# k^T v of batches 2 to 7 made one batch per token tile instead of all in the first tile, in linear attention with a feed-forward layer

## The chip, the cores and the metric

The kernel runs on one core of a Trainium2 chip. The metric is the device time of one execution in microseconds (us); less is better. The core's engines work side by side, each through its own list of instructions in order: TensorE (PE, with its weight loads as PEld), VectorE (DVE), ScalarE (ACT), GpSimd (POOL), and SyncE (SP), which here issues nearly all DMAs. They wait for each other by semaphores. Matrix products land in PSUM; ACT and DVE carry them on to SBUF.

## The reference

q, k, v have the shape (8 batches, 8 heads, 576 positions, 64), all float32. For each batch and head:

```python
kv = np.einsum('bhsd,bhse->bhde', k, v)
out = np.einsum('bhsd,bhde->bhse', q, kv)
rms = np.sqrt(np.mean(out * out, axis=-1, keepdims=True) + 1e-06)
x = out / rms * g_norm            # then heads side by side: (4608, 512)
h = x @ w_in                      # w_in (512, 2048)
g = h * np.tanh(softplus(h))      # "Mish"
return g @ w_out                  # w_out (2048, 512)
```

w_in and w_out are float64 in memory, so the kernel reads them as pairs of 32-bit words and builds float32 values from them.

## The kernel before

**Tiles and slots.** The 4608 tokens are cut into nine tiles of 512 (NT = 9). A tile lies over one or two batches (576 positions each), which `segments(j)` tells. The first half of the kernel makes h and g of every tile and stores g in DRAM (`gd`); the second half loads g and multiplies it with w_out. Both products use a scheme in which a 2 by 2 block product takes seven multiplications of blocks (A11, S1, ... with B11, T1, ...) instead of eight. Each factor is split into a high and a low part of the fast matmul type, and each product is three matmuls (low by high, high by low, high by high). In the first half one multiplication is 12 matmuls of 128x128 by 128x256 (L478) and fills one *slot*. A tile has four groups of seven, so NS = 28 slots; tile i has the slots 28 i to 28 i + 27.

**A plan by slots.** The order is written out by hand. `at(t, f)` puts a piece of work behind the product of slot t, `then(t, f)` ahead of it; `slot` runs both lists. Within a slot the pieces run in the order in which they were registered, and every engine and SP's DMA queue keep that order. A slot below zero is put at slot 0. What comes before slot 0 is a preamble, written line by line.

**w_in.** It comes in eight chunks j, each of four DMAs of 256 KB (L135) into one buffer (`w64`, a single one; chunk 1 has a room of its own). Then SCALE (ACT, L140), JOIN (three DVE instructions, L145 to L147, after which the buffer is free for the next load), DIFF (DVE, L155 to L157), BLOCKS and SUMS (casts on ACT, L118, with a subtraction on DVE, L119). A chunk j from 2 on has LOAD at slot 3(j-2)-2 (chunk 2's is in the preamble), SCALE and JOIN at 3(j-2), DIFF and BLOCKS one later, SUMS two later. Group n of tile 0 needs the chunks 2n and 2n+1. w_out is converted in 16 pieces of the same steps, from tile 1 on, every 12 slots.

**k^T v.** `kv_product` makes the product of one or two pairs of heads: 20 float32 matmuls with 64 columns each per pair (L233), into one PSUM bank `kvps`, whose halves go by the batch's parity. Batch 0 is done in the preamble. The 28 pairs of batches 1 to 7 stand at slots 0 to 20 of tile 0; each pair needs four DMAs (`km`, `kr`, `vm`, `vr`, L212 and L213) into one of two buffers (`kvp`), and the load of a pair is issued two pairs ahead. `kv_keep` copies a finished batch to SBUF with ACT (L245). `kv_store` then puts it into DRAM (`kvd`), and from tile 2's attention on, `kv_fetch` and `kv_split` bring it back and split it into a high and a low part.

**Attention.** The attention of tile j runs during tile j-1, in two units of four heads: load of q (8 DMAs, L286), transpose (DVE, L291), halves (the split), project (q by k^T v, L314 or L317 to L319), square, scaled, squares, sums (L349 to L352), rstd (ACT), keep and spread (rstd to DRAM and back, spread over partitions, L367 and L374), normalize (DVE, L382). `x_form` then makes the split left factors of the next tile (slots 24 to 32). Tiles 0 and 1 (T32 = 2) use plain float32 matmuls, which need no halves.

**Stores.** `put_in` applies Mish on ACT and stores g two or three slots later from SP (L496, L501, L504).

The names and lines that matter below: `kv_keep`, `kv_store`, `kv_fetch`, `kv_split` (L243 to L258), `project` (L304), the preamble (L528 to L590), the planned slots of w_in and of k^T v (L593 to L604), `attention` (L606), and the slots of w_out's conversion (L651 to L661).

Of the kernel before, what the change touches and what calls it, by code (L numbers as in the profile page):

```python
# [26 lines left out]
def linear_attention_rms_mish_ffn(  # L27
# [33 lines left out]

# [32 lines left out]
    kvs = part1.enter_context(tc.tile_pool(name="kvs", bufs=1))  # L94
    xp = part1.enter_context(tc.tile_pool(name="xp", bufs=1))
# [13 lines left out]
    kvd = [tc.dram_tile([P, NKC, P], F32, name=f"kvd{b}") for b in range(B)]  # L109
# [107 lines left out]
    def kv_staging():  # L217
        ts = []
        for name in ("k", "v"):
            ts.append(pools["kvp"].tile([P, 2, CM * D], F32, name=f"{name}m"))  # L220
            ts.append(pools["kvp"].tile([SL, 2, D], F32, name=f"{name}r"))
        return ts
# [14 lines left out]
    kvf = [kvs.tile([P, 2, NKC, P], F32, name=f"kv{n}") for n in range(2)]  # L237
    kvt = {}

    def kv_room(b):  # L240
        return kvf[0][:, b] if b < 2 else kvf[1][:, b % 2]

    def kv_keep(b, n):  # L243
        for r in (slice(0, D), slice(D, P)):
            nc.scalar.copy(kv_room(b)[r, n, r], kvps[r, b % 2, n, :])  # L245

    def kv_store(b):
        nc.sync.dma_start(kvd[b], kv_room(b))

    raw = {}  # L250

    def kv_fetch(b):
        raw[b] = kvs.tile([P, NKC, P], F32, name="kvr")
        nc.sync.dma_start(raw[b], kvd[b])

    def kv_split(b):
        kvt[b] = kvs.tile([P, 2, NKC, P], F32R, name=f"kv{b % 2}")
        split(kvt[b][:, 0], kvt[b][:, 1], raw[b])  # L258
# [14 lines left out]
    def unit_steps(j, u):  # L273
# [30 lines left out]
        def project():  # L304
# [208 lines left out]
    open_pools(wst, ("w64", 1), ("wd", 1), ("kvp", 2))  # L513
# [32 lines left out]
    staged = []  # L546
# [351 lines left out]
```

## Time and profile before

| | us |
|---|---|
| median of 3 runs (957.92 to 959.98) | 958.29 |
| the profiled execution | 959.49 |
| its span, first to last instruction | 957.7 |
| PE busy | 853.3 (89%) |
| DVE busy | 610.0 (64%) |
| ACT busy | 463.2 (48%) |
| DMA of SP's queue, share of 16 engines | 61.1% |

The page's second part cuts the span into 40 slices of 24 us. A digit is the busy share of the slice in tenths; PEclk is the clock that TensorE was granted, in the same tenths:

```profile
PE   3468758999979999997989969999999999999997
DVE  2476442768668676748585515886766777667762
ACT  1444333666646666655666525444444434444341
PEclk9667978999999999998999989999999999999999
DMA  9478987667659768765873799634544345443331
```

The first slot begins in the second slice, the second half of the kernel at about the 25th (587 us). In a row of the timeline, the first number is the start, the second the length, both in us; several instructions of one line are merged (x12), and in brackets stand the idle time ahead and what ended it. "SPq" is a DMA being issued by SP, not its transfer. In a row of groups, "busy, mean ns of one" and the idle time before it follow after the bars.

### The profile page before, as it was taken

What the parts mean: (1) busy time and instruction counts of PE and PEld (TensorE: products, weight loads), DVE (VectorE), ACT (ScalarE), POOL (GpSimd) and SP (SyncE); (2) the same over time, 40 slices, a digit from 0 to 9 for tenths busy, and PEclk for the clock granted to TensorE, in tenths of its full rate; (3) what the DMA queues carried; (4) which work ended last, traced back from release to release, by engine and by line L of the source; (5) the groups of instructions that cost most, each with busy time, mean ns of one, the idle gap of its engine ahead of it and who ended that gap; (6) DMA issues with size and microseconds to landing.
All of it is one profiled execution on the core that took longest, in us unless ns stands there. A gap on an engine that the chain in (4) does not pass through costs nothing.

```text
span 957.7 us, 17048 instructions
## 1 busy us (share of the span) xinstructions
PE 853.3 (89%) x6940; PEld 811.8 (85%) x6940; DVE 610.0 (64%) x801; ACT 463.2 (48%) x703; POOL 3.4 (0%) x19
## 2 busy tenths in 40 slices
PE   3468758999979999997989969999999999999997
PEld 1156546989879989887989969999999999999997
DVE  2476442768668676748585515886766777667762
ACT  1444333666646666655666525444444434444341
POOL 1000000000000000000000000000000000000000
PEclk9667978999999999998999989999999999999999
DMA  9478987667659768765873799634544345443331
GB/s 250 114 197 231 268 257 216 225 203 234 190 171 276 221 181 255 221 184 155 241 208 132 244 405 367 217 111 141 165 124 123 110 120 168 134 130 110 111 111 45
DMA packets 159150, 181.08 MB, mean 189 GB/s; under 512 B 18976, under 2 KB 138784, under 8 KB 158048
## 3 DMA queue, kind: packets, MB, share of 16 engines
q1 hardware_dynamic: 155872, 177.64, 61.1%
q10 hardware_dynamic: 3200, 2.36, 1.0%
q8 instruction: 54, 0.88, 0.4%
q14 instruction: 24, 0.20, 0.1%
HBM read 116.13 MB, written 63.83 MB: 188 GB/s over the span
## 4 chain that ended last, share of the span: by engine, by line
PE 62%; DMA 12%; DVE 11%; ACT 7%; SPq 4%; issue 3%; ACTq 0%; DVEq 0%
PE a L726 20%; PE bc L726 15%; PE a L478 11%; PE bc L478 7%; DMA vm<-in_v_dram 3%; DMA gd<-ula 3%; PE q L808 2%; PE s L233 2%; DMA w<-in_moe_w_in_dram 2%; DMA gd<-ur 2%; DMA qs<-in_q_dram 2%; DVE ur L498 1%; DVE fl L119 1%; ACT gf L118 1%; SPq L135 1%
## 5 line engine op out<-in xcount | busy, mean ns | idle before, releaser
L726 PE MATMUL a<-wf,gf 128*128 128x256 f32 x1632 | 201.8, 283 | 0.5 <-DVE ur L757 0.5
L726 PEld LDWEIGHTS a<-wf,gf 128*128 128x128 f32 x1632 | 198.4, 192 | 0.7 <-DVE ur L757 0.7
L478 PE MATMUL a<-gf,wf 128*128 128x256 f32 x1296 | 179.9, 295 | 17.2 <-DVE gf L380 10.9
L478 PE MATMUL bc<-gf,wf 128*128 128x256 f32 x1296 | 176.8, 291 | 15.0 <-DVE ula L498 7.6
L119 DVE TENSOR_TENSOR gf<-g,gf 128x1024 fp32r<-128x1024 f32 (+1 forms) x123 | 132.9, 1087 | 87.9 <-ACT gf L118 87.8
L478 PEld LDWEIGHTS a<-gf,wf 128*128 128x128 f32 x1296 | 169.3, 201 | 21.7 <-issue 11.7
L478 PEld LDWEIGHTS bc<-gf,wf 128*128 128x128 f32 x1296 | 167.1, 197 | 17.5 <-issue 9.0
L118 ACT CAST gf<-g 128x1024 fp32r<-128x1024 f32 (+1 forms) x123 | 114.5, 939 | 90.5 <-DVE g L706 65.3
L726 PE MATMUL bc<-wf,gf 128*128 128x256 f32 x1224 | 152.6, 283 | 0.1
L726 PEld LDWEIGHTS bc<-wf,gf 128*128 128x128 f32 x1224 | 149.4, 192 | 0.3 <-ACT gf L118 0.3
L478 PEld LDWEIGHTS a<-a,wf 128*128 128x128 f32 x432 | 57.3, 199 | 9.1 <-DVE ur L498 4.8
L115 ACT ACTIVATE ur<-ur 128x1024 f32<-128x1024 f32 x36 | 38.1, 1058 | 53.4 <-DVE ur L498 53.4
L478 PE MATMUL a<-a,wf 128*128 128x256 f32 x432 | 61.0, 293 | 1.9 <-DVE ur L498 1.8
L233 PE MATMUL s<-vm,km 128*64 128x64 f32 x448 | 24.3, 266 | 32.7 <-DMA vm<-in_v_dram 20.7
L233 PEld LDWEIGHTS s<-vm,km 128*64 128x64 f32 x448 | 20.1, 172 | 37.6 <-DMA vm<-in_v_dram 10.3
L498 DVE TENSOR_TENSOR ula<-bc,ula 128x512 f32<-128x512 f32 x36 | 24.7, 686 | 35.6 <-PE bc L478 18.2
L446 ACT COPY ur<-bc 128x512 f32<-128x512 f32 (+1 forms) x53 | 27.5, 518 | 39.2 <-PE bc L726 23.0
L118 ACT CAST gf<-gf 128x512 fp32r<-128x512 f32 x45 | 27.8, 618 | 38.2 <-DVE gf L404 18.2
L118 ACT CAST gf<-a 128x1024 fp32r<-128x1024 f32 x17 | 17.9, 1051 | 53.4 <-DVE a L703 53.4
L119 DVE TENSOR_TENSOR gf<-gf 128x512 fp32r<-128x512 f32 x45 | 31.0, 689 | 17.3 <-ACT gf L118 16.7
L455 ACT COPY ur<-a 128x512 f32<-128x512 f32 (+1 forms) x53 | 27.4, 517 | 30.2 <-PE a L726 24.6
L119 DVE TENSOR_TENSOR fl<-fa,fh 128x1024 fp32r<-128x1024 f32 x28 | 34.1, 1219 | 9.4 <-ACT fh L118 9.4
(129 smaller groups left out, 867.7 us busy)
## 6 DMA issues: line engine op xcount, KB each, us to landing
g<-gd SPq DMA_DIRECT2D x18, 2048.0 KB, 8.7
gd<-ur SPq DMA_DIRECT2D x36, 512.0 KB, 5.1
wod<-wst SPq DMA_DIRECT2D x16, 896.0 KB, 5.4
wf<-wod SPq DMA_DIRECT2D x8, 1792.0 KB, 15.0
gd<-ula SPq DMA_DIRECT2D x36, 256.0 KB, 4.4
gd<-ulb SPq DMA_DIRECT2D x36, 256.0 KB, 4.6
w<-in_moe_w_out_dram SPq DMA_DIRECT2D x32, 256.0 KB, 5.1
w<-in_moe_w_in_dram SPq DMA_DIRECT2D x28, 256.0 KB, 4.5
```

The costliest lines, as they stand in the source:

```text
L115: nc.scalar.activation(o, i, AF.Mish)
L118: nc.scalar.copy(hi, src)
L119: nc.vector.tensor_sub(lo, src, hi.bitcast(F32))
L135: nc.sync.dma_start(dst, src)
L233: nc.tensor.matmul(kvps[o * D:(o + 1) * D, b % 2, h0 // 2 + i, :], kt, vt, start=(c == 0), stop=(c == CM))
L446: then(t + 2, lambda: nc.scalar.copy(dst(st, "22"), st["c"]))
L455: then(t + 4, lambda: nc.scalar.copy(dst(st, "12"), st["a"]))
L478: nc.tensor.matmul(bank[:, jj], w[:, right, a, kc, :], xf[:, b, kc, :], start=first and jj == kc == s == 0, stop=(kc == 1 and s == 2), ski ...
L498: nc.vector.tensor_add(o, bank, o)
L726: nc.tensor.matmul(bank, gf[:, a, c, :], wo[c][:, right, b, :], start=first and c == s == 0, stop=(c == NF2 - 1 and s == 2), skip_group_ch ...
L808: nc.tensor.matmul(banks[b][:, h], gf[:, a, c, :], wo[2 * n + c][:, right, d, :], start=n == c == s == h == 0, stop=last_one, skip_group_c ...
```

## The change

- k^T v of batch 1 stays at the start of tile 0, one pair per slot (0 to 3). Batch b from 2 on has its four pairs at the slots 13, 16, 19 and 22 of tile b-2, that is, two tiles ahead of the attention which first needs it. Its first two loads are issued at slots 20 and 23 of the tile before (batch 2: at 4 and 6), the other two at 14 and 17.
- `kv_keep` writes the split parts straight from PSUM at slot 24 (slot 4 for batch 1); the trip through DRAM (`kv_store`, `kv_fetch`, `kv_split`) is gone. Batches 0 and 1 have their float32 tiles in the pool `kvf`, which closes with tile 0; the staging buffers `kvp` stay open.
- w_in: SCALE and JOIN of chunk 2 move from the preamble into slot 0, and the load of chunk j+1 is at slot 3(j-2)+1, as before, but chunk 2's stands earlier in SP's order. In the preamble w_in's first load stands ahead of k's and v's, DIFF and SUMS of chunk 0 stand earlier, and g_norm's load stands later.
- Attention: q's first load at -19 (was -18), transpose at -1 (0), halves at 0 (1), the second unit's load at 1 (2), keep at 17 (18), spread at 19 (20), normalize at 24 and 25 (23 and 24), the x forms at 25 to 30 and 32 (24, 25 and 28 to 32). For tile 1's attention the steps ahead of 19 come two slots later.
- w_out's conversion begins two slots later (NS+6 instead of NS+4), and its loads are 13 slots ahead instead of 16.

```diff
@@ -92,6 +91,7 @@
     ps_t = part1.enter_context(tc.tile_pool(name="ps_t", bufs=1, space=PSUM))
     att = part1.enter_context(tc.tile_pool(name="att", bufs=1))
     kvs = part1.enter_context(tc.tile_pool(name="kvs", bufs=1))
+    kvp = part1.enter_context(tc.tile_pool(name="kvp", bufs=2))
     xp = part1.enter_context(tc.tile_pool(name="xp", bufs=1))
     wst = part1.enter_context(ExitStack())
     pools = {}
@@ -106,7 +106,6 @@
     sel = const.tile([P, NKC, H], F32R, name="sel")
     gd = [tc.dram_tile([P, NFC, T], F32, name=f"gd{i}") for i in range(NT)]
     wod = [tc.dram_tile([P, 7, 2, G], F32, name=f"wod{c}") for c in range(NF2)]
-    kvd = [tc.dram_tile([P, NKC, P], F32, name=f"kvd{b}") for b in range(B)]
     rd = [tc.dram_tile([H, T], F32, name=f"rd{j}") for j in range(NT)]
 
     ctx.enter_context(tc.manual_schedule(engines=None))
@@ -217,8 +216,8 @@
     def kv_staging():
         ts = []
         for name in ("k", "v"):
-            ts.append(pools["kvp"].tile([P, 2, CM * D], F32, name=f"{name}m"))
-            ts.append(pools["kvp"].tile([SL, 2, D], F32, name=f"{name}r"))
+            ts.append(kvp.tile([P, 2, CM * D], F32, name=f"{name}m"))
+            ts.append(kvp.tile([SL, 2, D], F32, name=f"{name}r"))
         return ts
 
     kvps = ps_t.tile([P, 2, NKC, D], F32, name="s2")
@@ -234,28 +233,23 @@
 
 
 
-    kvf = [kvs.tile([P, 2, NKC, P], F32, name=f"kv{n}") for n in range(2)]
-    kvt = {}
-
-    def kv_room(b):
-        return kvf[0][:, b] if b < 2 else kvf[1][:, b % 2]
+    kvf, kvt = [], []
+
+    def kv_tiles():
+        for n in range(T32):
+            kvf.append(pools["kvf"].tile([P, NKC, P], F32, name=f"kvf{n}"))
+            nc.gpsimd.memset(kvf[n], 0.0)
+        for n in range(2):
+            kvt.append(kvs.tile([P, 2, NKC, P], F32R, name=f"kv{n}"))
+            nc.gpsimd.memset(kvt[n].bitcast(F32), 0.0)
 
     def kv_keep(b, n):
         for r in (slice(0, D), slice(D, P)):
-            nc.scalar.copy(kv_room(b)[r, n, r], kvps[r, b % 2, n, :])
-
-    def kv_store(b):
-        nc.sync.dma_start(kvd[b], kv_room(b))
-
-    raw = {}
-
-    def kv_fetch(b):
-        raw[b] = kvs.tile([P, NKC, P], F32, name="kvr")
-        nc.sync.dma_start(raw[b], kvd[b])
-
-    def kv_split(b):
-        kvt[b] = kvs.tile([P, 2, NKC, P], F32R, name=f"kv{b % 2}")
-        split(kvt[b][:, 0], kvt[b][:, 1], raw[b])
+            if b < T32:
+                nc.scalar.copy(kvf[b][r, n, r], kvps[r, b % 2, n, :])
+        for r in (slice(0, D), slice(D, P)):
+            if b >= T32 - 1:
+                split(kvt[b % 2][r, 0, n, r], kvt[b % 2][r, 1, n, r], kvps[r, b % 2, n, :])
 
 
     def segments(j):
@@ -311,9 +305,9 @@
                 ps, hp = st["x"][a], 2 * u + a
                 for b, _, c in segments(j):
                     if j < T32:
-                        nc.tensor.matmul(ps[:, c], kvf[0][:, b, hp, :], st["q"][:, a, c], start=True, stop=True)
+                        nc.tensor.matmul(ps[:, c], kvf[b][:, hp, :], st["q"][:, a, c], start=True, stop=True)
                         continue
-                    kh, kl, qh, ql = kvt[b][:, 0, hp, :], kvt[b][:, 1, hp, :], st["qh"][:, a, c], st["ql"][:, a, c]
+                    kh, kl, qh, ql = kvt[b % 2][:, 0, hp, :], kvt[b % 2][:, 1, hp, :], st["qh"][:, a, c], st["ql"][:, a, c]
                     nc.tensor.matmul(ps[:, c], kl, qh, start=True, stop=False)
                     nc.tensor.matmul(ps[:, c], kh, ql, start=False, stop=False)
                     nc.tensor.matmul(ps[:, c], kh, qh, start=False, stop=True)
@@ -510,7 +504,7 @@
         for s in steps:
             units[j][u][s]()
 
-    open_pools(wst, ("w64", 1), ("wd", 1), ("kvp", 2))
+    open_pools(wst, ("w64", 1), ("wd", 1), ("kvf", 1))
     rooms = [up.tile([P, 4, CM * D], F32, name="ur") for _ in range(2)]
     rooms += [x[:, 2 * u:2 * u + 2].rearrange("p a (h n) -> p (a h) n", h=2) for u in range(2)]
     rrooms = [up.tile([SL, 4, D], F32, name=n) for n in ("ula", "ula", "ulb", "ulb")]
@@ -525,15 +519,20 @@
         for s in steps:
             conv[j][s]()
 
-    kv0 = [kv_load(nc.scalar, 0, 4 * n, 4, [t for m in range(2) for t in (rooms[2 * n + m], rrooms[2 * n + m])]) for n in range(2)]
+    staged = {}
+
+    def k_load(b, p):
+        staged[b, p] = kv_load(nc.sync, b, 2 * p, 2, kv_staging())
+
+    def k_product(b, p):
+        kv_product(b, 2 * p, 2, *staged.pop((b, p)))
+
     nc.scalar.preload_act_table_set("natural_log_exp_and_others")
     weights(0, LOAD)
+    kv0 = [kv_load(nc.scalar, 0, 4 * n, 4, [t for m in range(2) for t in (rooms[2 * n + m], rrooms[2 * n + m])]) for n in range(2)]
     do(0, 0, "load")
     weights(1, LOAD)
-    for r in (slice(0, D), slice(D, P)):
-        nc.sync.dma_start(gcol[r, :], g_norm.rearrange("(p o) -> p o", o=1))
-    for t in kvf:
-        nc.gpsimd.memset(t, 0.0)
+    kv_tiles()
     nc.gpsimd.memset(eps, 1e-6)
     nc.gpsimd.memset(ones, 0.0)
     nc.gpsimd.memset(ones[0:D, 0:D], 1.0)
@@ -543,37 +542,24 @@
         for o in range(2):
             nc.gpsimd.memset(sel[o * D:(o + 1) * D, hp, 2 * hp + o:2 * hp + o + 1].bitcast(F32), 1.0)
 
-    staged = []
-    order_kv = [(b, h0) for b in range(1, B) for h0 in range(0, H, 2)]
-
-    def kv_next_load():
-        if order_kv:
-            b, h0 = order_kv.pop(0)
-            staged.append((b, h0, kv_load(nc.sync, b, h0, 2, kv_staging())))
-
-    def kv_next_product(t):
-        b, h0, ts = staged.pop(0)
-        kv_product(b, h0, 2, *ts)
-        if h0 == H - 2:
-            then(t + 1, lambda: kv_keep(b, slice(0, NKC)))
-            at(t + 3, lambda: kv_store(b))
-
     weights(0, SCALE, JOIN)
     kv_product(0, 0, 4, *kv0[0])
     kv_keep(0, slice(0, 2))
+    weights(0, DIFF)
     do(0, 0, "transpose")
     do(0, 1, "load")
-    kv_next_load()
-    kv_next_load()
-    weights(0, DIFF)
+    for r in (slice(0, D), slice(D, P)):
+        nc.sync.dma_start(gcol[r, :], g_norm.rearrange("(p o) -> p o", o=1))
+    weights(2, LOAD)
+    k_load(1, 0)
     do(0, 0, "project")
+    weights(0, BLOCKS)
     kv_product(0, 4, 4, *kv0[1])
     kv_keep(0, slice(2, 4))
-    weights(0, BLOCKS)
     do(0, 0, "square", "sums")
+    weights(0, SUMS)
     do(0, 1, "transpose", "project", "square")
-    weights(0, SUMS)
-    weights(2, LOAD)
+    k_load(1, 1)
     do(0, 0, "rstd")
     do(0, 1, "sums")
     weights(1, SCALE, JOIN)
@@ -586,7 +572,6 @@
     x_form(S1)
     weights(1, SUMS)
     x_form(S2)
-    weights(2, SCALE, JOIN)
     x_form(A12)
 
 
@@ -595,70 +580,56 @@
     at(2, lambda: x_form(A22))
     for j in range(2, NF2):
         t = 3 * (j - 2)
-        for s, n in ((LOAD, -2), (SCALE, 0), (JOIN, 0), (DIFF, 1), (BLOCKS, 1), (SUMS, 2)):
-            if j > 2 or s >= DIFF:
-                at(max(t + n, 0), lambda j=j, s=s: weights(j, s))
-    for n in range(len(order_kv) + len(staged)):
-        t = n * 6 // 8
-        at(t, lambda t=t: kv_next_product(t))
-        at(t, kv_next_load)
+        if j + 1 < NF2:
+            at(t + 1, lambda j=j: weights(j + 1, LOAD))
+        for s, n in ((SCALE, 0), (JOIN, 0), (DIFF, 1), (BLOCKS, 1), (SUMS, 2)):
+            at(t + n, lambda j=j, s=s: weights(j, s))
+
+
+    for p in range(4):
+        if p > 1:
+            at(p - 2, lambda p=p: k_load(1, p))
+        at(p, lambda p=p: k_product(1, p))
+    at(4, lambda: kv_keep(1, slice(0, NKC)))
+    for b in range(2, B):
+        t = NS * (b - 2)
+        for p in range(4):
+            at(t + (4, 6, 14, 17)[p] if b == 2 else t + (20 - NS, 23 - NS, 14, 17)[p], lambda b=b, p=p: k_load(b, p))
+            at(t + (13, 16, 19, 22)[p], lambda b=b, p=p: k_product(b, p))
+        at(t + 24, lambda b=b: kv_keep(b, slice(0, NKC)))
 
     def attention(j):
 
-        t = NS * (j - 1)
-        if T32 <= j:
-            for b in ((j - 1, j) if j == T32 else (j,)):
-                if b < B:
-                    at(t - 14 if b > T32 else t - 16 if b == T32 else t - 4, lambda b=b: kv_fetch(b))
-                    at(t - 9 if b > T32 else t - 12 if b == T32 else t, lambda b=b: kv_split(b))
-
-        def steps(u, n, *names):
-            if t + n >= 0:
-                at(t + n, lambda: do(j, u, *names))
-            else:
-                at(0, lambda: do(j, u, *names))
-        steps(0, -18, "load")
-        steps(0, 0, "transpose")
-        steps(0, 1, "halves")
-        steps(1, 2, "load")
-        steps(0, 3, "project")
-        steps(0, 5, "square", "scaled")
-        steps(0, 6, "squares")
-        steps(1, 7, "transpose")
-        steps(0, 8, "sums")
-        steps(1, 9, "halves")
-        steps(1, 11, "project")
-        steps(1, 12, "square", "scaled")
-        steps(1, 13, "squares")
-        steps(1, 15, "sums")
-        steps(1, 16, "rstd")
-        steps(1, 18, "keep")
-        steps(0, 20, "spread0")
-        steps(0, 23, "normalize")
-        steps(1, 24, "normalize")
-        for f, n in zip(MADE, (24, 25, 28, 29, 30, 31, 32)):
-            at(t + n, lambda f=f: x_form(f))
-
-    for j in range(1, NT):
-        r = units[j][1]["rstd"]
-
-        def spread0(j=j):
+        def spread():
             units[j][0]["spread"]()
             units[j][1]["spread"]()
-        units[j][0]["spread0"] = spread0
+        units[j][0]["spread0"] = spread
+        t = NS * (j - 1)
+        late = 2 if j == 1 else 0
+        for u, n, *names in (
+            (0, -19, "load"), (0, -1, "transpose"), (0, 0, "halves"), (1, 1, "load"), (0, 3, "project"),
+            (0, 5, "square", "scaled"), (0, 6, "squares"), (1, 7, "transpose"), (0, 8, "sums"), (1, 9, "halves"),
+            (1, 11, "project"), (1, 12, "square", "scaled"), (1, 13, "squares"), (1, 15, "sums"), (1, 16, "rstd"),
+            (1, 17, "keep"), (0, 19, "spread0"), (0, 24, "normalize"), (1, 25, "normalize"),
+        ):
+            at(max(t + n + (late if n < 19 else 0), 0), lambda u=u, names=names: do(j, u, *names))
+        for f, n in zip(MADE, (25, 26, 27, 28, 29, 30, 32)):
+            at(t + n, lambda f=f: x_form(f))
+
+    for j in range(1, NT):
         attention(j)
 
     def out_pools():
         wst.close()
         open_pools(wst, ("w64", 2), ("wx", 1), ("wst", 1))
-    at(NS - 3, out_pools)
+    at(NS - 2, out_pools)
     for i in range(2 * NF2):
-        for s, n in zip(range(7), (-16, 0, 0, 1, 2, 3, 6)):
+        for s, n in zip(range(7), (-13, 0, 0, 1, 2, 3, 6)):
             def run(i=i, s=s):
                 if s == 0:
                     conv["out", i] = weight_out(i // 2, i % 2)
                 conv["out", i][s]()
-            at(max(NS - 2, NS + 4 + 12 * i + n), run)
+            at(max(NS - 2, NS + 6 + 12 * i + n), run)
 
 
     wo = [None] * NF2
```

More of the change, by code (lines that the diff above doesn't have):

```diff
@@ L606, in attention @@
     def attention(j):
+        def spread():
+            units[j][0]["spread"]()
+            units[j][1]["spread"]()
+        units[j][0]["spread0"] = spread
         t = NS * (j - 1)
-        if T32 <= j:
-            for b in ((j - 1, j) if j == T32 else (j,)):
-                if b < B:
-                    at(t - 14 if b > T32 else t - 16 if b == T32 else t - 4, lambda b=b: kv_fetch(b))
-                    at(t - 9 if b > T32 else t - 12 if b == T32 else t, lambda b=b: kv_split(b))
-        def steps(u, n, *names):
-            if t + n >= 0:
-                at(t + n, lambda: do(j, u, *names))
-            else:
-                at(0, lambda: do(j, u, *names))
@@ L640, in attention @@
+        for f, n in zip(MADE, (25, 26, 27, 28, 29, 30, 32)):
             at(t + n, lambda f=f: x_form(f))
     for j in range(1, NT):
-        r = units[j][1]["rstd"]
-        def spread0(j=j):
-            units[j][0]["spread"]()
-            units[j][1]["spread"]()
-        units[j][0]["spread0"] = spread0
         attention(j)
```

## The prediction

> **What bounds the kernel now.** I read the page's slices first (a low granted clock and a nearly full DMA row in the first sixth, a full PE row after it), then the timeline of PE to find where each token tile begins. Tile 0 runs from 47.77 to 176.66, tiles 1 to 7 to 535.41, tile 8 to 587.12. (The products of L478 come in twelves, so the 28th slot can be counted off.) The view of busy time by stretch, cut there, gives:
>
> ```profile
> core 0: us, PE busy (x) PEld busy (x) DVE busy (x) ACT busy (x) POOL busy (x), PEclk, DMA share, GB/s
> 47.77:176.66 128.89, 95.59 (x909) 79.55 (x910) 67.22 (x90) 50.26 (x77) 0.00 (x0) 0.78 0.85 242
> 176.66:535.41 358.75, 332.11 (x2566) 316.49 (x2565) 250.06 (x381) 226.22 (x357) 0.00 (x0) 0.98 0.69 205
> 587.12:957.70 370.58, 365.04 (x3036) 364.46 (x3036) 258.11 (x278) 151.50 (x210) 0.00 (x0) 1.00 0.44 136
> ```
>
> Tile 0 takes 128.89 us; a later tile takes 358.75 / 7 = 51.25 us for the same 28 slots. Later tiles and the second half are TensorE: 332 of 359 us and 365 of 371 us busy. So there are two regimes, and the change moves work from the one with idle PE into the one without. What does PE wait for in tile 0? The view of the k^T v line (L233) says it, followed by the line's own busy time by stretch:
>
> ```profile
> its engine sat idle before it (us, times) until:
>   DMA vm<-in_v_dram: 31.1, 14
> ...
>   ACT kv L245: 12.7, 2
> ```
>
> ```profile
> 47.77:176.66 128.89, 33.28 (x560) 26.76 (x560) 0.78 0.85 242
> ```
>
> (The idle times count PE and its weight loads apart, so 31.1 is some 20 of time.) All 28 head pairs of batches 1 to 7 stand here, and they wait for their loads. But a second chain lies under this one: w_in's loads have one buffer, so each chunk goes load, SCALE (L140), JOIN (L145 to L147), and only then the next load. Here are chunks 3 and 4, then chunk 7's SCALE, from the timeline:
>
> ```profile
> 57.00 1.22 DVE L147 SCALAR_TENSOR_TENSOR fl<-w,fl 128x1024 uint32<-128x1024 uint32 x1
> 60.81 1.92 SPq L135 DMA_DIRECT2D w<-in_moe_w_in_dram  x4
> 69.87 1.16 ACT L140 ACTIVATE fl<-w 128x1024 f32<-128x1024 f32 x1
> 73.05 1.23 DVE L147 SCALAR_TENSOR_TENSOR fl<-w,fl 128x1024 uint32<-128x1024 uint32 x1
> 78.29 0.61 SPq L213 DMA_DIRECT2D vr<-in_v_dram  x1
> 79.01 2.07 SPq L135 DMA_DIRECT2D w<-in_moe_w_in_dram  x4
> 85.91 1.12 ACT L140 ACTIVATE fl<-w 128x1024 f32<-128x1024 f32 x1 [2.17 <-DMA w<-in_moe_w_in_dram]
> 89.04 1.22 DVE L147 SCALAR_TENSOR_TENSOR fl<-w,fl 128x1024 uint32<-128x1024 uint32 x1
> 113.72 4.85 SPq L286 DMA_DIRECT2D qs<-in_q_dram  x8
> 137.72 1.12 ACT L140 ACTIVATE fl<-w 128x1024 f32<-128x1024 f32 x1 [4.39 <-DMA w<-in_moe_w_in_dram]
> ```
>
> From issue to SCALE is 85.91 - 79.01 = 6.9; from SCALE to the end of JOIN is 90.26 - 85.91 = 4.35. The load was free to go at 74.28 and went at 79.01: SP was issuing k and v pieces until 78.90. So chunk 3's SCALE to chunk 7's SCALE took 67.85 us, of which 4 x (6.9 + 4.35) = 45 is the chain itself and the rest waiting in SP's queue. ACT's queue is in order, so evictions stand behind SCALE and PE cannot run more than a slot or two past it. This chain is what is late next.
>
> **Tile 0 after the change.** Preamble: w_in chunk 0's SUMS moves ahead of unit 1's steps, SCALE/JOIN of chunk 2 moves behind slot 0, w_in's first DMAs go out ahead of k's and v's and the table load ahead of ACT's issues. The one thing on the chain is SUMS' cast, which stood between unit 1's square and rstd:
>
> ```profile
> 35.19 1.05 ACT L118 CAST wf<-wd 128x1024 fp32r<-128x1024 f32 x1
> ```
>
> So slot 0 comes about 1 earlier; DIFF's three DVE subtractions now stand ahead of the first transpose, so I keep -2 to +2. kv_tiles clears 3072 instead of 2048 columns on POOL, which has nothing else to do; gcol's two issues move behind q's and are used twenty us later: both nothing, and a us at most without that cover.
>
> In the slots: S4's three steps now come before chunk 2's JOIN, which therefore ends near 61, not at 58.22; but chunk 3's load waited on SP until 60.81 anyway, behind the second k/v pair and q, so it goes at about the same time, and with less traffic I put its SCALE at 67.5 (was 69.87). From there four cycles of 10.8 (6.25 with a quieter queue, 4.35, 0.2 of pick-up) make 43.2. One new delay: q's load for tile 2 moves from slot 10 to 9, so its 8 issues (4.85 above) now stand on SP ahead of chunk 6's load at slot 10, and wait for a transpose that stands behind JOIN: +5.5. Chunk 7's SCALE: 67.5 + 43.2 + 5.5 = 116, against 137.72. The k/v loads that remain (two of batch 1 at slots 0 and 1, batch 2 at 4, 6, 14, 17) stand behind w_in's load of their slot or have no load near.
>
> From that SCALE to tile 1:
>
> ```profile
> 139.51 1.12 PE L233 MATMUL s<-vm,km 128*64 128x64 f32 x16 [5.35 <-ACT ur L446]
> ...
> 141.16 1.12 PE L233 MATMUL s<-vm,km 128*64 128x64 f32 x16
> ...
> 142.62 3.57 PE L349 MATMUL ss<-fa,sel 128*8 128x512 f32 x4
> ...
> 172.34 3.04 PE L478 MATMUL bc<-gf,wf 128*128 128x256 f32 x24
> 175.22 3.04 PE L478 MATMUL a<-gf,wf 128*128 128x256 f32 x24
> ```
>
> and, for a head pair between two products at full clock:
>
> ```profile
> 79.50 0.69 PE L233 MATMUL s<-vm,km 128*64 128x64 f32 x16
> ...
> 80.38 1.69 PE L478 MATMUL bc<-gf,wf 128*128 128x256 f32 x12
> ```
>
> Two products take 2.88 (172.34 to 175.22), so 1.44 each; a pair takes 80.38 - 79.50 = 0.88 at full clock, and 1.65 (139.51 to 141.16) after a gap of 5.35, when the clock is low. PE resumes 1.8 after SCALE, at 118; 12 products 17.3, three pairs of batch 2 2.6, the sums at slot 17 1.8 (half of 3.57), and 3.3 for the slow start (the 6.6 us from 139.51 to the first product after the sums ran at about half speed): tile 1 begins near 143, against 176.66. **Tile 0: -33.6.**
>
> The Trainium skill, TensorE: Matmul & The Clock Gate, Part 1, says an idle window of about 3.4 us halves the clock and about as much sustained work restores it; by that the slow start would cost 1.7 and the tile 1.6 less. The trace agrees in direction (1.65 against 0.88 for one pair) but the slow stretch was longer, and I take the row.
>
> The spread of rstd is nearly as late: store to DRAM, load back, normalize.
>
> ```profile
> 161.37 0.49 SPq L367 DMA_DIRECT2D rd<-fa  x1
> 168.48 1.22 DVE L382 TENSOR_TENSOR gf<-gf,fh 128x1024 f32<-128x1024 f32 x1 [2.68 <-DMA fh<-rd]
> ```
>
> That is 7.1. With the sums at slot 17 and normalize at slot 24, about 12 of PE lie between; it fits with 1 or 2 to spare, so 0 here, 3 if SP is late.
>
> **Tiles 1 to 7.** Batches 3 to 7 bring 20 pairs of 0.88 into a saturated PE: **+17.5**. At the slow clock it would be 33, but these tiles were granted 0.98. Traffic, from the view of DMA issues (KB each, then us to landing):
>
> ```profile
> km<-in_k_dram SPq DMA_DIRECT2D x28, 256.0 KB, 3.6
> vm<-in_v_dram SPq DMA_DIRECT2D x28, 256.0 KB, 4.2
> ...
> kvr<-kvd SPq DMA_DIRECT2D x7, 256.0 KB, 5.0
> kr<-in_k_dram SPq DMA_DIRECT2D x28, 32.0 KB, 3.8
> vr<-in_v_dram SPq DMA_DIRECT2D x28, 32.0 KB, 3.5
> ```
>
> A pair is 576 KB in four DMAs, a batch 2.36 MB; five batches less the dropped kvd trips raise 205 GB/s to some 223, below tile 0's 242. Of each batch, pairs 2 and 3 are loaded (slots 14, 17) only when pairs 0 and 1 (13, 16) have freed the two buffers, and used at 19 and 22. The load needs four issues of some 0.6 and is complete about 6 after the first (1.2 + 4.2 for vm, 1.8 + 3.5 for vr); between pair 0 and pair 2 lie six products and one pair, 9.5. Margin about 3.5, eaten only if SP is held: I take +1 in all, 0 to 12.
>
> kv_keep, nearest rows:
>
> ```profile
> 166.58 0.75 ACT L245 COPY kv<-s 64x256 f32<-64x256 f32 x2 [12.38 <-PE s L233]
> L119 DVE TENSOR_TENSOR wst<-wx,wst 128x256 fp32r<-128x256 f32 x16 | 6.7, 418 | 0.0
> L119 DVE TENSOR_TENSOR kv<-kvr,kv 128x512 fp32r<-128x512 f32 x6 | 4.1, 686 | 6.3 <-ACT kv L118 6.3
> ```
>
> Its two subtractions (2 x 0.42) replace one of 0.69 but now stand at slot 24, ahead of normalize and the x forms, where DVE is dense: +2 over six tiles, 0 to 5. The waits of PE in tiles 1 to 7:
>
> ```profile
> PE bc L478 <- DVE ula L498: 7.6, 2, 3.9
> PE x L318 <- DVE fl L119: 7.1, 7, 1.6
> ```
>
> The second is project waiting for the halves of q, which now come a slot (1.44) earlier: up to -7, I take -3, since DVE's work at the tile's start is the same. The first stands at the start of tiles 3 and 6, where a w_out conversion fell at slot 24 of the tile before, on top of the x forms. All conversions move by two, so these fall at 26, and another pair moves from 20 to 22, into normalize: +3, from -4 to +8. The normalize steps and x forms one slot later keep three slots to their products: 0.
>
> **Sum.** -33.6 + 17.5 + 1 + 2 - 3 + 3 = -13.1 against the span of 957.7. The profiled execution took 959.49, the median of the runs is 958.29; the parts outside the span don't change, so I take it from the median: **945**. Tile 8 and the second half keep their order.
>
> **Rivals.**
> (1) *Better:* w_in's cycle is 9.9 (load to SCALE 5.3) and q's issues hide: SCALE 7 at 107, tile 1 at 133, -44; and the pairs fill a part of PE's 26.6 idle us in tiles 1 to 7, so +17.5 becomes +14: 928. For it: tile 0's DVE is busy 67 of 129 only. Against: issue plus landing has hardly been below 6.
> (2) *Slower:* w_in's chain keeps its pace because the wait in SP's queue only changes its cause (q's issues, stores that wait for Mish): chunks at 14 to 16 us, chunk 7's SCALE at 131. Then tile 0 gives 7 plus about 11 from the five pairs fewer behind it, -18 against +20.5: 961. It decides once tile 0 saves less than 20. For it: 60.81 and 79.01, loads late through SP. Against: what stood ahead of them was mostly k and v. The Trainium skill, Perfetto Trace Analysis, Identifying the Most-Contended Engine, speaks for this side: it wants the busiest engine relieved first, and from tile 1 on that is the engine that gets the pairs.
> (3) *Late loads:* pairs 2 and 3 wait 2 us each in five tiles, +20 at most with the clock falling behind such gaps: 955 to 968, say 960. For it: L233's 14 waits in tile 0 with the same two buffers. Against: there the lead was one or two slots, here five.
>
> **How the numbers follow.** Forecast 0.62 (its own range 935 to 955), rival 1 0.14, rival 2 0.12, rival 3 0.12. A change of 0.2% (1.9 us) is about what a measurement can tell here. Faster than 956.4: 0.62 + 0.14 + 0.02 + 0.02 = 0.80; same: 0.04 + 0.05 = 0.09; slower: 0.06 + 0.05 = 0.11. Range 928 to 961: about 0.07 lies below, 0.09 above.
>
> **What would show it.** Right: tile 0 near 96 us with SCALE of w_in 10 to 11 apart, a larger step before chunk 6, hardly a wait on vm; tiles 1 to 5 about 3.5 to 4 longer, tiles 6 and 7 within 1.5 of before; L233 busy near 0.9 a pair in later tiles. Wrong: SCALEs 14 or more apart (rival 2), waits of L233 on vm in tiles 1 to 5 (rival 3), a wait on DVE over 5 us at the tiles' starts, or tiles 1 to 5 no longer than before (rival 1).

## The result, and the profile after

| | before | changed |
|---|---|---|
| median of 4 runs, us | 958.11 (957.28 to 959.98) | 949.69 (948.55 to 950.33) |
| ratio, 95% interval | | 0.9908 (0.9891 to 0.9926) |
| profiled span | 957.7 | 946.8 |
| preamble, up to slot 0 | 47.77 | 46.31 |
| tile 0 | 128.89 | 91.32 |
| tiles 1 to 7 | 358.75 | 386.90 |
| tile 8 and second half | 422.3 | 422.3 |

The changed kernel is 0.9% faster: 8.4 us, where 13 were forecast. In the two profiled spans 39.0 us are gained up to the start of tile 1 (33.6 forecast), and 28.2 are given back in tiles 1 to 7 (20.5 forecast). The slices of the page after:

```profile
PE   2457598989799898979989979999999999999997
...
PEclk9769799999899899998999989999999999999999
DMA  9465666877869578668665799445443345443331
```

DMA's row has come down in the first fifth, and the busy stretch of PE begins earlier; but PEclk now has four 8s from the 11th slice to the 24th, where before it had two. The forecast did not have that. The view of busy time by stretch, cut at the changed kernel's own tile starts (tile 0, then tiles 1 to 7), and then the line of k^T v (L232 here) in the same stretches:

```profile
46.31:137.63 91.32, 64.39 (x509) 55.79 (x509) 64.48 (x89) 44.67 (x66) 0.00 (x0) 0.82 0.61 175
137.63:524.53 386.90, 356.69 (x2966) 338.64 (x2965) 253.11 (x389) 230.05 (x363) 0.00 (x0) 0.96 0.73 220
```

```profile
46.31:137.63 91.32, 8.95 (x160) 7.14 (x160) 0.82 0.61 175
137.63:524.53 386.90, 18.93 (x400) 14.83 (x400) 0.96 0.73 220
```

Tiles 1 to 7 have 24.6 more of busy TensorE than before (356.7 against 332.1), of which the pairs account for 18.9, and 3.6 more of idle time. The other 5.7 of busy time is the same matmuls at a lower granted clock: 0.96 against 0.98. What TensorE waited for there, from the view of waits in that stretch:

```profile
PE a L472 <- DVE ur L492: 25.6, 8, 5.5
PE bc L472 <- DVE gf L118: 2.4, 7, 0.3
PE bc L472 <- ACT gf L117: 1.7, 3, 1.0
PE a L472 <- ACT ur L449: 0.5, 1, 0.5
```

The list of before had 7.6 for the addition `ula` and 7.1 for project. It also had these two:

```profile
PE ss L351 <- DVE fl L119: 5.1, 7, 1.7
PE a L478 <- DVE ur L498: 1.0, 2, 0.5
```

The first three are gone. The last, 1.0 in all, has become 25.6: 2.73 in each of tiles 1, 2, 4, 5 and 7, and 5.50 in tiles 3 and 6, where a conversion of w_out stands at slot 26 just ahead. It is the product of slot 30 (A22 of the tile before, added onto bank a), and it waits for the addition of slot 28, which carries the sum so far out of that bank. The timeline of DVE and of PE around the start of tile 1:

```profile
140.79 0.68 DVE L396 TENSOR_TENSOR gf<-s,gf 128x512 f32<-128x512 f32 x1
142.16 0.69 DVE L118 TENSOR_TENSOR gf<-gf 128x512 fp32r<-128x512 f32 x1 [0.69 <-ACT gf L117]
142.77 1.24 DVE L285 STREAM_TRANSPOSE fa<-qs 128x1024 f32<-128x1024 f32 x1
143.93 0.65 DVE L492 TENSOR_TENSOR ur<-a,ur 128x512 f32<-128x512 f32 x1
```

```profile
144.63 2.80 PE L472 MATMUL a<-a,wf 128*128 128x256 f32 x12 [2.73 <-DVE ur L492]
147.23 2.04 PE L472 MATMUL a<-gf,wf 128*128 128x256 f32 x12
```

The two subtractions of S2 (L396 and L118), the wait for the cast between them and the transpose now stand at slot 27 and thus, on DVE, ahead of the addition of slot 28 (the row at 143.93). Before, that addition stood ahead of all of them, and the product of slot 30 did not wait:

```profile
176.85 0.69 DVE L498 TENSOR_TENSOR ur<-a,ur 128x512 f32<-128x512 f32 x1 [0.75 <-PE a L478]
177.46 0.68 DVE L402 TENSOR_TENSOR gf<-s,gf 128x512 f32<-128x512 f32 x1
...
180.04 1.24 DVE L291 STREAM_TRANSPOSE fa<-qs 128x1024 f32<-128x1024 f32 x1
```

```profile
179.53 1.60 PE L478 MATMUL a<-a,wf 128*128 128x256 f32 x12
```

And the product behind the new wait takes 2.80, almost what two undisturbed ones take (3.04 in the rows of before). The stretches of 2 us there show why; the third figure from the end of each row is the granted clock:

```profile
142.00:144.00 2.00, 0.00 (x0) 0.00 (x0) 1.84 (x3) 0.64 (x2) 0.00 (x0) 1.00 0.80 279
144.00:146.00 2.00, 1.37 (x7) 1.37 (x8) 2.00 (x4) 1.96 (x3) 0.00 (x0) 0.70 0.29 70
146.00:148.00 2.00, 2.00 (x11) 2.00 (x11) 1.32 (x3) 1.54 (x5) 0.00 (x0) 0.50 0.82 240
148.00:150.00 2.00, 2.00 (x17) 2.00 (x16) 1.01 (x2) 1.79 (x5) 0.00 (x0) 0.94 0.93 221
```

The clock is whole or half. In tiles 1 to 7 the trace's clock records put 34 us at half clock, where before had 14 (2 x (1 - 0.96) x 387 = 31 and 2 x (1 - 0.98) x 359 = 14 from the rows).

In tile 0 the chain of w_in is as forecast; the SCALEs of chunks 3 to 7, from the timeline:

```profile
65.87 1.12 ACT L139 ACTIVATE fl<-w 128x1024 f32<-128x1024 f32 x1 [3.21 <-DMA w<-in_moe_w_in_dram]
...
76.67 1.16 ACT L139 ACTIVATE fl<-w 128x1024 f32<-128x1024 f32 x1
...
87.83 1.12 ACT L139 ACTIVATE fl<-w 128x1024 f32<-128x1024 f32 x1 [1.89 <-DMA w<-in_moe_w_in_dram]
...
105.22 1.12 ACT L139 ACTIVATE fl<-w 128x1024 f32<-128x1024 f32 x1 [9.29 <-DMA w<-in_moe_w_in_dram]
...
115.87 1.13 ACT L139 ACTIVATE fl<-w 128x1024 f32<-128x1024 f32 x1 [0.74 <-DMA w<-in_moe_w_in_dram]
```

From SCALE to SCALE these are 10.8, 11.2, 17.4 and 10.7 us: the step ahead of chunk 6 is the long one.

### The profile page after: what moved, and what is told of

It is laid out like the page before. It is cut to its first block, busy times and chain, and to the rows that moved or that the text cites. A ratio compares the mean times of both kernels' runs of the same rounds, so it can differ in the third digit from the quotient of the medians.

```text
span 946.8 us, 17029 instructions
## 1 busy us (share of the span) xinstructions
PE 846.3 (89%) x6940; PEld 809.7 (86%) x6940; DVE 610.7 (64%) x808; ACT 461.2 (49%) x698; POOL 4.3 (0%) x21
## 5 line engine op out<-in xcount | busy, mean ns | idle before, releaser
L118 DVE TENSOR_TENSOR gf<-g,gf 128x1024 fp32r<-128x1024 f32 (+1 forms) x123 | 132.9, 1087 | 87.9 <-ACT gf L117 87.9
L472 PE MATMUL bc<-gf,wf 128*128 128x256 f32 x1296 | 174.7, 287 | 11.3 <-ACT ur L440 6.6
L472 PEld LDWEIGHTS bc<-gf,wf 128*128 128x128 f32 x1296 | 164.3, 194 | 16.8 <-ACT ur L440 6.8
L472 PE MATMUL a<-a,wf 128*128 128x256 f32 x432 | 68.2, 314 | 38.5 <-DVE ur L492 38.5
L472 PEld LDWEIGHTS a<-a,wf 128*128 128x128 f32 x432 | 63.1, 217 | 44.0 <-DVE ur L492 41.0
L440 ACT COPY ur<-bc 128x512 f32<-128x512 f32 (+1 forms) x53 | 27.4, 517 | 39.7 <-PE bc L697 23.0
L117 ACT CAST gf<-a 128x1024 fp32r<-128x1024 f32 x17 | 17.9, 1051 | 53.4 <-DVE a L674 53.4
L118 DVE TENSOR_TENSOR gf<-gf 128x512 fp32r<-128x512 f32 x45 | 30.9, 688 | 17.1 <-ACT gf L117 17.1
L449 ACT COPY ur<-a 128x512 f32<-128x512 f32 (+1 forms) x53 | 27.5, 518 | 29.2 <-PE a L697 24.6
L118 DVE TENSOR_TENSOR fl<-fa,fh 128x1024 fp32r<-128x1024 f32 x28 | 34.2, 1221 | 11.3 <-ACT fh L117 11.3
L117 ACT CAST fh<-fa 128x1024 fp32r<-128x1024 f32 x28 | 29.2, 1043 | 10.5 <-DVE fa L285 9.7
L114 ACT ACTIVATE ula<-ula 128x512 f32<-128x512 f32 x36 | 22.7, 630 | 22.0 <-DVE ula L492 21.9
```

The costliest lines, as they stand in the source:

```text
L114: nc.scalar.activation(o, i, AF.Mish)
L117: nc.scalar.copy(hi, src)
L118: nc.vector.tensor_sub(lo, src, hi.bitcast(F32))
L440: then(t + 2, lambda: nc.scalar.copy(dst(st, "22"), st["c"]))
L449: then(t + 4, lambda: nc.scalar.copy(dst(st, "12"), st["a"]))
L472: nc.tensor.matmul(bank[:, jj], w[:, right, a, kc, :], xf[:, b, kc, :], start=first and jj == kc == s == 0, stop=(kc == 1 and s == 2), ski ...
```

## The experiments

Two theories stood at the start. *Order*: the extra time in tiles 1 to 7 comes from what now stands on DVE ahead of the addition at slot 28, once as a wait and once as halved clock. *Pairs*: it comes from the 20 pairs themselves. All times below are medians beside runs of the kernel before on the same chip (957.56, 957.51 and 956.65 in the three sets); the lengths of tiles 1 to 7 are from the profiled run, as is the granted clock there. The changed kernel's own 949.69 is from the first measurement. Slot 0 came between 44.8 and 48.4 with the same preamble, so single us of the whole time say little and the tiles' lengths more. The profiled run is one of those behind the median: e2's was 3.4 us below it, x1's 5.7 and b1's 4.5 above.

| run | us | tile 0 | tiles 1 to 7 | clock in 1 to 7 |
|---|---|---|---|---|
| before | 958.11 | 128.9 | 358.8 | 0.98 |
| changed | 949.69 | 91.3 | 386.9 | 0.96 |
| e1_transpose_0 | 947.46 | 93.5 | 384.6 | 0.97 |
| e2_s2_28 | 946.13 | 90.7 | 381.9 | 0.99 |
| e3_attention_before | 938.61 | 87.5 | 381.3 | 1.00 |
| e5_no_pairs | 934.75 | 91.6 | 374.1 | 0.95 |
| e6_q_behind_w | 944.58 | 86.6 | 387.4 | 0.96 |
| e9_filler | 944.76 | 90.7 | 381.6 | 0.99 |
| e7_att_conv_before | 942.91 | 87.5 | 383.4 | 0.99 |
| e8_att_pairs_early | 932.40 | 87.5 | 375.3 | 0.99 |
| c1_before_new_slots | 960.94 | 125.8 | 364.5 | 0.96 |
| x1_att_no_pairs | 914.78 | 89.3 | 359.1 | 1.00 |
| b1_early_s2 | 929.76 | 87.3 | 376.6 | 1.00 |
| b2_conv_placed | 926.56 | 87.5 | 369.8 | 1.00 |

**One piece of the order at a time.** First the transpose alone:

```diff
-(0, -1, "transpose"), (0, 0, "halves"), (1, 1, "load"),
+(0, 0, "transpose"), (0, 1, "halves"), (1, 2, "load"),
```

> The changed kernel with the first unit's transpose, halves and second q load back at slots 0, 1 and 2 of the tile. Theory (order): in the changed kernel S2's form and the transpose stand at slot 27, on DVE ahead of the addition at slot 28 that empties bank a, so the product of slot 30 waits 2.73 in each tile (5.50 in two), and the granted clock is halved for one or two stretches of 3.4 us behind it. Without the transpose (1.24) ahead of it the wait falls to about 1.5 and most of the slow stretches go: tiles 1 to 7 shorter by 7 x 1.24 plus 3 to 5 of clock, 10 to 14 us less than the changed kernel (about 936 to 940). Rival (pairs): the 20 pairs cost more than 0.88 each in the later tiles and DVE is late in sum whatever its order: within 2 us of the changed kernel's 949.7, the wait only moves to project.

then S2, with the three forms behind it, one slot later each:

```diff
-zip(MADE, (25, 26, 27, 28, 29, 30, 32))
+zip(MADE, (25, 26, 28, 29, 30, 31, 32))
```

> The changed kernel with the forms S2, A12, S4, S3 and A22 at slots 28, 29, 30, 31 and 32 instead of 27, 28, 29, 30 and 32. Theory (order): S2's addition, the wait for its cast and its subtraction (2.0 together) no longer stand ahead of the addition at slot 28, so the wait at slot 30 falls from 2.73 to about 0.7 and the slow clock behind it goes: 7 x 2.0 plus 4 to 6, so 16 to 20 us less than the changed kernel (930 to 934), unless S2 itself, needed at slot 31, is late then (half of it given back). Rival (pairs): within 2 us of 949.7.

The wait itself moved as the theory says: at the start of tile 1 from 2.73 to 1.60 and to 0.75. But the time hardly followed: tiles 1 to 7 are 2.3 and 5.0 shorter, and the whole 2.2 and 3.6, against 10 to 14 and 16 to 20 expected. Both expectations failed in size, and the first run comes close to its rival (within 2 us, and the wait moves to project). The view of waits in tiles 1 to 7 shows where the time went, first for the transpose moved back, then for S2:

```profile
PE a L472 <- DVE ur L492: 17.7, 8, 4.4
PE x L312 <- DVE fl L118: 4.5, 7, 0.9
```

```profile
PE a L472 <- ACT ula L435: 12.0, 7, 1.9
PE a L472 <- DVE ur L492: 11.7, 8, 3.5
```

One piece less ahead of the addition, and the next thing that DVE or ACT owes is late: project's halves in the one, the copy out of bank a in the other. So theory *order* held for where the wait is, not for what a single piece is worth: the start of a tile is dense, and the pieces share one delay.

**All of the order.** The table of attention as before for tiles 2 to 8, everything else as changed:

```diff
-(0, -19, "load"), (0, -1, "transpose"), (0, 0, "halves"), (1, 1, "load"), ...
-(1, 17, "keep"), (0, 19, "spread0"), (0, 24, "normalize"), (1, 25, "normalize"),
+(0, -18, "load"), (0, 0, "transpose"), (0, 1, "halves"), (1, 2, "load"), ...
+(1, 18, "keep"), (0, 20, "spread0"), (0, 23, "normalize"), (1, 24, "normalize"),
-zip(MADE, (25, 26, 27, 28, 29, 30, 32))
+zip(MADE, (24, 25, 28, 29, 30, 31, 32))
```

> The changed kernel with all slots of attention and x forms of tiles 2 to 8 as in the kernel before; only k^T v, the preamble, w_in's and w_out's slots stay changed. Theory (order): tiles 1 to 7 take the 358.75 of before plus 20 pairs of 0.97 (19.4), some 378 against 386.9, so 8 to 9 less than the changed kernel: 941. Rival (pairs): 949.7 within 2.

938.6, 11 less than the changed kernel, so not the rival. Tiles 1 to 7 give 5.6 of it, where 8 to 9 were expected, at a clock of 1.00. Tile 0 gives most of the rest, because q's load for tile 2 is back behind w_in's load here; that move alone:

```diff
-at(max(t + n + (late if n < 19 else 0), 0), ...
+at(max(t + n + (late if n < 19 else 0) + (1 if (j, n) == (2, -19) else 0), 0), ...
```

> The changed kernel with one move: q's first load for tile 2 stands at slot 10 of tile 0 again, behind the load of w_in's chunk 6, not at slot 9 ahead of it. Theory (w_in's chain sets tile 0): the SCALE of chunk 6 follows that of chunk 5 by about 11 us, not 17.4, and tile 0 ends 5 to 6.5 earlier: 943 to 945. Rival (DVE or the k and v loads set tile 0): chunk 6 comes earlier but tile 1 starts within 2 us of 137.6.

Chunk 6's load and SCALE in that run, behind chunk 5's SCALE at 90.45:

```profile
94.89 1.91 SPq L134 DMA_DIRECT2D w<-in_moe_w_in_dram  x4
...
102.22 1.16 ACT L139 ACTIVATE fl<-w 128x1024 f32<-128x1024 f32 x1 [3.67 <-DMA w<-in_moe_w_in_dram]
```

11.8 from SCALE to SCALE where the changed kernel took 17.4, tile 0 4.8 shorter (86.55), the whole 5.1. The chain of w_in sets tile 0.

**Without the pairs** (both kernels leave k^T v of batches 3 to 7 out of the computation), first with the changed kernel's slots, then with attention's slots of before (e3's base):

```diff
-for p in range(4):
+for p in range(4 if b == 2 else 0):
     at(..., lambda b=b, p=p: k_load(b, p))
     at(..., lambda b=b, p=p: k_product(b, p))
```

> The changed kernel without loads and products of k^T v of batches 3 to 7 (left out of the computation; the copies out of the bank stay). Theory (order): the pairs cost 0.9 to 1.0 each and nothing else, so 18 to 20 less than the changed kernel (930 to 932), and the waits at slot 30 stay at 2.73 and 5.50 with their slow clock. Rival (pairs): they carry all of the 28 us that tiles 1 to 7 gained, so 26 to 30 less (920 to 924), and the waits at slot 30 go with them.

> As e3_attention_before (attention and x forms at the slots of before), without loads and products of k^T v of batches 3 to 7 (left out of the computation). Theory: with the clock whole the pairs cost what TensorE spends on them and no more, 20 x 0.8 to 0.97: tiles 1 to 7 at 362 to 366 instead of 381.3, 919 to 923 in all. Rival (a part of the pairs is hidden in waits that stay): 12 to 13 less than e3, as between the changed kernel and e5_no_pairs: 925 to 927.

The changed slots without pairs take 374.1 in tiles 1 to 7; here too, tile 1's product of slot 30 waits, and is slow behind the wait:

```profile
144.26 2.93 PE L472 MATMUL a<-a,wf 128*128 128x256 f32 x12 [2.74 <-DVE ur L492]
```

With attention's slots of before they take this:

```profile
137.62:496.67 359.05, 328.91 (x2566) 313.32 (x2565) 253.55 (x390) 228.25 (x363) 0.00 (x0) 1.00 0.67 203
```

359.05, beside the 358.75 of before. So the four tile lengths are: neither 359.1; slots alone 374.1 (+15.0); pairs alone 381.3 (+22.2); both 386.9 (+27.9). The two do not add up. A likely reason, which no run here shows by itself, is that each pair ahead of the tile's start also gives DVE time to catch up, and that a part of the pairs fills time in which TensorE waits anyway. Neither theory was right alone, and both runs missed both of their ranges. In e5 the pairs were worth 12.8 in the tiles and 15 in all, less than either theory gave, and the wait at slot 30 stayed (27.4 in all), as *order* said. In x1 they were worth 22.2 in the tiles, more than the 18.9 for which they keep TensorE busy, and 914.8 lies below both ranges.

The equality with before has two unequal parts. Tile 1, whose own x forms keep their changed slots in e3 and x1, takes 53.4 in x1 where before took 48.9. Tiles 2 to 7 take 305.6 where before took 309.8. The other edits that reach them, conversions two slots later and the copies out of the bank at slot 24 in place of `kv_fetch` and `kv_split`, thus cost nothing there in sum.

**The order alone, in the kernel before:**

```diff
 (in the kernel before, for j > 1)
-steps(0, -18, "load")
-steps(0, 0, "transpose")
+steps(0, -19, "load")
+steps(0, -1, "transpose")
...
-zip(MADE, (24, 25, 28, 29, 30, 31, 32))
+zip(MADE, (25, 26, 27, 28, 29, 30, 32))
```

> The kernel before, with nothing changed but the slots of attention and of the x forms for tiles 2 to 8, which are those of the changed kernel; k^T v stays in tile 0. Theory (the order at a tile's start costs by itself): the wait at slot 30 on the addition that empties bank a appears here too, about 2.7 in most tiles, with halved clock behind it, and tiles 2 to 7 take 6 to 12 more in all: 964 to 970. Rival (the order costs only together with the pairs and kv_keep): 957 to 960.

960.94, ratio 1.0041 (1.0021 to 1.0060): slower than before beyond its interval, but short of the theory's 964 to 970 and just above the rival's 960. Tiles 1 to 7 take 364.50 instead of 358.75, at 0.96 instead of 0.98, and the wait is there:

```profile
PE a L478 <- DVE ur L498: 16.2, 9, 3.2
```

Tile 0 came 3.1 shorter in that run, for which no cause was looked for. So the same move of slots has three prices in tiles 1 to 7: 5.8 here, 5.6 in the changed kernel with its pairs, and 15.0 in the changed kernel without them. Between the first and the last, both without pairs in these tiles, the conversions' slots, the copies at slot 24 and the forms of tile 1 differ; no run separates them.

**What the halved clock costs.** The wait stays, TensorE is kept at work in it:

```diff
+def filler():
+    d = ps_t.tile([P, 2, T], F32, name="x2")
+    for _ in range(20):
+        nc.tensor.matmul(d[:, 0, 0:TH], wf[0][:, 0, 0, 0, :], xforms[A22][:, 0, 0, :], start=True, stop=True)
+for j in range(1, NT - 1):
+    at(NS * j + 1, filler)
```

> The changed kernel with 20 matmuls of 256 columns more (2.4 us at full clock, into a bank that nothing reads) behind the product of slot 29 of tiles 1 to 7, where TensorE waits for the addition that empties bank a. Theory (the wait is paid twice, once as idle time and once as halved clock behind it): the filler takes idle time alone in five tiles, the halved stretches in tiles 1 to 7 go from 34 us to 14 or less, and the time falls by 5 to 9: 941 to 945. Rival (the granted clock does not depend on this wait): halved stretches as before and the time equal or up to 3 longer.

944.76, 4.9 less, as the theory had it, with 140 matmuls more whose result nobody reads. The start of tile 1:

```profile
142.30 2.56 PE L625 MATMUL x<-a,wf 128*128 128x256 f32 x20
145.19 1.69 PE L472 MATMUL a<-a,wf 128*128 128x256 f32 x12 [0.33 <-DVE ur L492]
```

The product behind the filler takes 1.69, not 2.80; the clock in tiles 1 to 7 rises to 0.99 (7 us halved in place of 34, at the starts of tiles 3 and 6), and those tiles are 5.3 shorter. So of the 28 us given back, some 5 were the clock behind the new wait.

**Towards a better kernel.** Conversions of w_out back to their old slots, on e3's base:

```diff
-(-13, 0, 0, 1, 2, 3, 6) ... NS + 6 + 12 * i + n
+(-16, 0, 0, 1, 2, 3, 6) ... NS + 4 + 12 * i + n
```

> As e3_attention_before, and w_out's conversion back at its slots of the kernel before (first at 32, loads 16 ahead). Theory (order): with the conversions where before had them, tiles 1 to 7 come near 358.75 plus 16 to 19 for the pairs, 375 to 378 instead of 381.3: 933 to 936 in all. Rival (the two slots of the conversions do not matter, the pairs and kv_keep bring the rest): within 2 of e3's 938.6.

Both missed: 942.9, and tiles 1 to 7 at 383.4, 2.1 longer than e3's. The conversions' new slots were no loss with the pairs in place; why the old ones are worse there was not settled. Next, on e3's base again, the pairs of batches 3 to 7 six slots earlier and their copies at slot 18 (batch 3's first two loads stay where they were):

```diff
-(20 - NS, 23 - NS, 14, 17) ... (13, 16, 19, 22) ... t + 24
+(14 - NS, 17 - NS, 8, 11) ... (7, 10, 13, 16) ... t + 18
```

> As e3_attention_before, and the pairs of batches 3 to 7 six slots earlier (7, 10, 13, 16, copies out of the bank at 18 instead of 24). Theory (order): kv_keep's two subtractions and its casts no longer stand ahead of normalize, so the waits around the tile's start fall by up to 1.5 in tiles 1 to 4: 933 to 937. Rival (kv_keep is too short to matter): within 2 of e3's 938.6, or late loads at the new slots make it longer.

932.4: tiles 1 to 7 at 375.3, so the 20 pairs now cost 16.2 over x1, 0.81 each, which is less than their busy time (18.9 in 20 pairs). What moved was the copies with their subtractions and the pairs' place; which of the two gave more was not separated. On that base, S2 of tile 1 and the forms behind it move back as well, and then w_out's conversions move away from the start of the tile:

```diff
-(25, 26, 27, 28, 29, 30, 32)   (tile 1)
+(25, 26, 28, 29, 30, 31, 32)
```

> As e8_att_pairs_early, with the x forms of tile 1 too at 28 to 32 from S2 on. Theory: tile 1, the only one that still has S2 ahead of the addition at slot 28, loses its wait of 1.6 and gets 1 to 3 shorter than e8's 57.0: 930 to 932. Rival: the wait moves to another place of the same tile and the time is e8's 932.4 within 1.

```diff
+c = [NS * g + n for g in range(1, 8) for n in ((4, 12, 20) if g in (2, 5) else (6, 17))][i]
-zip(range(7), (-13, 0, 0, 1, 2, 3, 6)) ... at(max(NS - 2, NS + 6 + 12 * i + n), run)
+zip(range(7), (-11, 0, 0, 1, 2, 3, 6)) ... at(max(NS - 2, c + n), run)
```

> As b1_early_s2, with w_out's 16 conversions put by hand at slots 6 and 17 of a tile (4, 12 and 20 in tiles 2 and 5, loads 11 slots ahead), so that none falls on slots 24 to 31. Theory (DVE's density at the tile's start is what TensorE waits for): the waits that remain in tiles 3 and 6 and the halved stretches go, 2 to 5 less than b1: 926 to 930. Rival (the waits come from the order of the forms alone, not from the conversions): within 1 of b1.

b1: 929.8, and tile 1 1.2 shorter, both near the theory; but tiles 2 to 7 were 2.5 longer in the profiled run, which took 934.2, and the ratios to before (0.9720 for b1, 0.9740 for e8) have overlapping intervals. Whether this move gains is not settled. b2: 926.6, within its theory's range, ratio to before 0.968 (0.9658 to 0.9703), tiles 1 to 7 at 369.8:

```profile
132.25:502.03 369.78, 351.10 (x2967) 327.62 (x2965) 255.05 (x391) 228.16 (x363) 0.00 (x0) 1.00 0.77 231
```

The clock is whole, and the remaining waits of TensorE there are short, the largest groups being:

```profile
PE a L472 <- DVE ur L492: 7.3, 8, 1.5
PE x L312 <- DVE fl L118: 5.2, 7, 0.9
```

At 926.6, b2 beats both the kernel before and the changed one.

## Why the prediction was right, and where it was off

- *The sum:* the forecast of 945 came out 4.7 too low, and that near partly by luck: tile 1 began 5.4 earlier than forecast, and tiles 1 to 7 took 7.7 more, so two errors took most of each other away.
- *Two regimes, PE idle in the first:* right. Tile 0 gave 37.6 and the preamble 1.5, 39.0 together (forecast: 33.6 with the preamble's 1 in it).
- *w_in's chain is late next:* right. Chunk 7's SCALE came at 115.87 (forecast 116). That it agrees so closely is luck: chunk 3's SCALE came 1.6 early (65.87 for 67.5), and the four steps took 50.0 for 48.7. The step ahead of chunk 6 was 17.4 (forecast 10.8 + 5.5), and the experiment with q's load took most of the surplus away.
- *From that SCALE to tile 1:* 27 forecast, 21.8 measured. PE was not held until chunk 7's SCALE; it had been held at slot 16 by an addition that stood on DVE behind the work on chunk 6 (JOIN, which ended at 109.58, DIFF and a subtraction of BLOCKS), and went on earlier:

```profile
113.29 2.93 PE L472 MATMUL a<-a,wf 128*128 128x256 f32 x12 [10.59 <-DVE ur L492]
```

- *The loads that remain stand behind w_in's load of their slot or have no load near:* priced at nothing. Batch 1's last pair stands on SP behind chunk 3's load, which waits for JOIN, and PE waited 8.6 for it. The experiment with q's load had 10.0 of this wait and a tile 0 4.8 shorter, so it seems to have cost little beside the chain; no run took it away alone:

```profile
68.28 1.12 PE L232 MATMUL s<-vm,km 128*64 128x64 f32 x16 [8.62 <-DMA vm<-in_v_dram]
```

- *Late loads in tiles 1 to 7 (+1, a rival at 960):* they did not happen; no wait on vm is among TensorE's in tiles 1 to 7 of the changed kernel.
- *+17.5 for the pairs:* the price of one was right, 0.88 and in the best placing 0.81. What they add depends on what is late beside them: 12.8 with the changed slots, 22.2 with those of before, 16.2 in e8.
- *The tile's start (-3 for the halves, +3 for the conversions, +2 for kv_keep, 0 for the normalize steps and x forms):* here lies the error, 28.2 in place of 20.5 in tiles 1 to 7. The step that failed is "normalize steps and x forms one slot later keep three slots to their products: 0". It looked at who reads the forms, and not at what they now stand ahead of on DVE: the addition at slot 28. And only A11 and S1 had moved later; S2 and the three forms behind it had moved one slot earlier, S2 from 28 to 27, and the transpose from 28 to 27 with it, though the term of -3 took DVE's work at the tile's start to be the same. With these slots undone for tiles 2 to 8, tiles 1 to 7 gave back 5.6 of the 7.7; where the rest lies stays open. No wait of project is left, as forecast, but PE now comes to project later, behind the wait of 25.6, so the -3 can't be read off. The forecast's own sign of being wrong, a wait on DVE over 5 us at the tiles' starts, did show: 5.50 in tiles 3 and 6.
- *Clock:* the slow start after a gap was priced in tile 0 alone. The rule of the Trainium skill, TensorE: Matmul & The Clock Gate, Part 1, that an idle window of about 3.4 us halves the clock, bears on tiles 1 to 7 just as much. There, idle time of 1.8 to 3.1 us within 3.4 us was enough, less than the rule's figure, and the measurement decides.
- *Rivals:* better (928) and slower (961) were both away from the truth; w_in's steps of 11 and the 39.0 saved ruled out the second, tiles 1 to 5 at 55 to 57 the first, though the start of tile 1 lay about midway between the forecast's and the first rival's.

## What to carry to other kernels

When a step moves by a slot, look at what it now stands ahead of on its engine, above all at whatever empties a PSUM bank, and not only at who reads its result. Where an engine is dense, moving one piece shows the next one late, so undo pieces together before judging the cause, and do not add up what single pieces gave: the same move cost 5.6, 5.8 or 15.0 us here, by what stood beside it. And a repeated wait of two or three us on TensorE can be paid twice, the second time in the clock behind it.

## What the runs showed of the hardware

The granted clock is whole or half. In all fourteen traces its records change only at steps of 3.41 us on one even grid, and not where a wait begins or ends. In tiles 1 to 7, what halved a whole clock was how much of one such step TensorE sat idle. In the changed kernel it was idle for 2.73 us between 141.40 and 144.81, and the clock was 0.50 until 148.22; between 475.90 and 479.31 it was idle for 2.20 us, and again 0.50 followed. In e3, steps with 1.74 us (from 245.84) and 1.71 us (from 249.25) left the clock whole. Over tiles 1 to 7 of all fourteen traces, 1.8 us or more in a step at whole clock was always followed by half, less than 1.55 never, and in between both occurred (the ends of matmuls are modelled, so these figures are not sharp). So a wait of one length can halve the clock or not, by how it falls on the steps and what other waits lie beside it. Twenty matmuls whose result nobody reads, put into the wait, kept the clock whole at the starts of five of the seven tiles and saved 5 us.
